# Converting weight pieces two at a time: 1024 columns per operation in place of 512

## The chip, the cores and the metric

The kernel runs on one core of a Trainium2 chip. A core has five instruction streams that run side by side and wait for each other on semaphores: TensorE (PE in the profile; PEld is its weight loading), VectorE (DVE), ScalarE (ACT), GpSimd (POOL) and SyncE (SP, which here issues the transfers). The metric is device time in microseconds, the median of several runs; lower is better. The inputs of the three runs before are the same.

## The reference

Two blocks run one after the other. An attention without softmax, with 8 batches, 8 heads, 576 positions and 64 features per head, each row divided by its root mean square:

```
kv  = einsum('bhsd,bhse->bhde', k, v)
out = einsum('bhsd,bhde->bhse', q, kv)
out = out / sqrt(mean(out*out, -1) + 1e-6) * g_norm
```

and a feed-forward block on its 4608 rows of 512 features, with 2048 hidden features:

```
x = out.transpose(0, 2, 1, 3).reshape(4608, 512)
y = maximum(x @ w_in, 0)**2 @ w_out
```

The two weight matrices arrive as 64-bit floats, and the kernel must make 32-bit floats of them on the chip: it takes the two 32-bit words of each number as integers and puts sign, exponent and fraction together with shifts and masks.

## The kernel before, in words

The rows are worked through in nine strips of 512. Strip 0 is multiplied plainly, strip 1 with seven products in place of eight (sums of blocks of operands are prepared for that), later strips with two such levels. Everything is emitted by one Python program; each engine then executes its own instructions strictly in the order in which they were emitted, and the semaphore waits between engines are put in by a framework that tracks which stretch of a tile each instruction reads and writes.

**The weights.** There are 32 pieces of 128 x 512 numbers: pieces 0 to 15 of `w_in`, in four groups g of four (kc = 0 to 3), pieces 16 to 31 of `w_out`. A piece takes two operations on ScalarE (the magnitude of the high word into `w_c`, line 254; the low word shifted, in place in `raw`, line 258) and four on VectorE (clip, line 266; shift and mask, 268; sign, 272; the final integer add, 275, a custom instruction that writes the result). Pieces 0 to 3 are converted one by one among the work on the first strip (`first_piece`). The other 28 are converted in pairs, numbered here 2 to 15, by `convert_pieces`: ScalarE is one pair ahead, and on VectorE the eight operations of the two pieces alternate, so that no operation directly follows the one whose result it needs. Pairs 2 to 7 belong to `w_in`, 8 to 11 to the first half of `w_out` (`pieces_out`), 12 to 15 to its second half (`sums_out`), and behind each of these last four come eight subtractions of 256 columns (`minus`, line 292) and four stores of the sums to device memory (line 325).

**The result tile.** `w_in` has the layout `[partition, kh, g, block, 256 columns]`, with kh = 0 or 1, g = 0 to 3 and seven blocks; blocks 0 to 3 hold the four quarters of the weight, and blocks 4 to 6 sums and pieces of `w_out`. Within a partition all of kh = 0 lies ahead of all of kh = 1. A pair of `w_in` is one block range of one group g at both kh.

**The readers.** The up projection of strip 0 has 16 steps, called slots here (`up_first`, four slots for each g, 2 halves fh by 2 column blocks i). A slot multiplies four chunks of 128 input features (kc 0 to 3, in this order; kc % 2 is kh) into one of four PSUM buffers (tags A, B, A, C) at line 900, and ScalarE squares the positive part of the sum (lines 905 and 907) before the buffer can be used again four slots on. Slots 0 to 2 are finished early (`first_up`). The conversion of a pair is emitted between slots: pairs 2, 3, 4 and 5 behind slots 0, 1, 2 and 3, pairs 6 to 11 ahead of slots 4 to 9, pair 12 behind slot 11 and pairs 13 to 15 behind slots 13 to 15. ScalarE's two operations for pair n + 1 are emitted at the place of pair n.

**Buffers and queues.** `raw` has 8 buffers of one piece each, which the last four pairs share for their sums (`wt`); `w_c` has 4. Every load of a piece and every store goes through SP's one queue in program order; a load waits until its buffer is free.

Behind the up projection come the down projection of strip 0 (line 859, from 83.76 us), the sums `g_s` for it, and the sums of the weights for later strips (`w_t`), all of which VectorE does right behind the last pair.

Of the kernel before, what the change touches and what calls it, by code (L numbers as in the profile page):

```python
# [10 lines left out]
FP32 = mybir.dt.float32  # L11
I32 = mybir.dt.int32
U32 = mybir.dt.uint32
I64 = mybir.dt.int64
AF = mybir.ActivationFunctionType
ALU = mybir.AluOpType
# [4 lines left out]
def kernel(  # L21
# [34 lines left out]
    nc = tc.nc  # L56
    P = 128
# [4 lines left out]
    NP = H // 2  # L62
# [27 lines left out]
    c_pool = ctx.enter_context(tc.tile_pool(name="c", bufs=6))  # L90
    conv = ExitStack()
    xt_pool = conv.enter_context(tc.tile_pool(name="xt", bufs=1))
    raw_pool = conv.enter_context(tc.tile_pool(name="raw", bufs=8))
    spare_pool = conv.enter_context(tc.tile_pool(name="spare", bufs=1))
    wtmp = conv.enter_context(tc.tile_pool(name="wtmp", bufs=4))
    psums = ExitStack()
    fpsum = psums.enter_context(tc.tile_pool(name="fpsum", bufs=4, space=bass.MemoryType.PSUM))
    opening = ExitStack()
# [110 lines left out]
    def drip_queries():  # L209
# [5 lines left out]
    KH, FH, DH = NP // 2, d_ff // 2, d_model // 2  # L215
    FQ = FC // 2
    WN = 512
    NG = FQ // 2

    w_in = wpool.tile([P, KH, NG, 7, WN // 2], FP32, name="w_in")  # L220

    w_out = dram.tile([7, P, 2, FQ, P], FP32, name="w_out")
# [5 lines left out]
    w_out_11, w_out_21, w_out_t1 = w_first = [  # L228
        w_in[:, :, :, b].rearrange("p k g e -> p (k g) e") for b in (4, 5, 6)
    ]  # L230
    w_in_v = moe_w_in.rearrange("(kc p) (b g f) -> kc g p b f", p=P, b=2, g=NG)
    w_out_v = moe_w_out.rearrange("(b j p) (eh e) -> eh j p b e", p=P, b=2, eh=2)
    sources = [w_in_v[kc, g] for g in range(NG) for kc in range(NP)]
    sources += [w_out_v[eh, j] for eh in range(2) for j in range(FQ)]
    raw = []

    def load_piece():
        if len(raw) < len(sources):
            t = raw_pool.tile([P, 2, WN // 2], I64, name="raw", tag="raw")
            nc.sync.dma_start(out=t, in_=sources[len(raw)])  # L240
            raw.append(t)


    LEAST, MOST = 2.0**-15, float.fromhex("0x1.DFFFFEp+16")

    words, acted = {}, [0]

    def convert_on_act(i, parts=(0, 1)):
        view = lambda dt: raw[i].bitcast(dt).rearrange("p b (n two) -> p b n two", two=2)
        low, high, high_f = view(U32)[:, :, :, 0], view(I32)[:, :, :, 1], view(FP32)[:, :, :, 1]  # L250
        r = view(I32)[:, :, :, 0]
        if 0 in parts:
            c = wtmp.tile([P, 2, WN // 2], FP32, name="w_c", tag="w_c")
            nc.scalar.activation(c, high_f, AF.Abs)  # L254
            words[i] = c, r, high

        if 1 in parts:
            nc.scalar.activation(r, low, AF.Copy, scale=2.0**-29)  # L258

    def conversion(i, dest, eng=nc.vector):  # L260

        c, r, high = words.pop(i)
        ci = c.bitcast(I32)


        yield eng.tensor_scalar(out=c, in0=c, scalar1=LEAST, scalar2=MOST, op0=ALU.max, op1=ALU.min)

        yield nc.vector.tensor_scalar(
            out=ci, in0=ci, scalar1=3, scalar2=0x3FFFFFFF, op0=ALU.logical_shift_left, op1=ALU.bitwise_and
        )  # L270

        yield nc.vector.scalar_tensor_tensor(
            out=ci, in0=high, scalar=-(2**30), in1=ci, op0=ALU.bitwise_and, op1=ALU.bitwise_or
        )
        yield nc.vector.tensor_tensor(out=dest.bitcast(I32), in0=ci, in1=r, op=ALU.add)

    def convert_pieces(ids, dests):

        for i in range(acted[0], min(ids[-1] + 3, len(sources))):
            convert_on_act(i)  # L280
            acted[0] = i + 1
        for _ in zip(*[conversion(i, dest) for i, dest in zip(ids, dests)]):
            pass
        load_more(ids[-1] + 1)

    def load_more(end):

        while len(raw) < min(end + 8, max(len(sources) - 4, end + 4), len(sources)):
            load_piece()

    def minus(eng, out, a, b):
        eng.tensor_tensor(out=out, in0=a, in1=b, op=ALU.subtract)  # L292

    def pieces_in(i):
        g, kc = divmod(i, NP)
        b = kc // KH * 2
        convert_pieces((i, i + 1), [w_in[:, kh, g, b : b + 2] for kh in range(KH)])

    def sums_in(g):

# [5 lines left out]
        minus(nc.vector, a21, a11, a21)  # L306

    def pieces_out(j):
        dest = lambda j: w_in[:, j // NG, j % NG, 4:6]
        convert_pieces((NG * NP + j, NG * NP + j + 1), [dest(j), dest(j + 1)])  # L310

    def sums_out(j):
        js = (j, j + 1)
        t = [raw_pool.tile([P, 4, DH], FP32, name="wt", tag="raw") for _ in js]
        convert_pieces([NG * NP + FQ + j for j in js], [x[:, 0:2, :] for x in t])
        for x, j in zip(t, js):
            minus(nc.vector, w_out_t1[:, j, :], x[:, 0], w_out_11[:, j, :])
        for x, j in zip(t, js):
            minus(nc.vector, x[:, 2], x[:, 1], w_out_t1[:, j, :])
        for x in t:  # L320
            minus(nc.vector, x[:, 0], x[:, 1], x[:, 0])
        for x, j in zip(t, js):
            minus(nc.vector, x[:, 3], w_out_21[:, j, :], x[:, 2])
            for e in range(2):
                nc.sync.dma_start(out=w_out[3:7, :, e, j].rearrange("b p e -> p b e"), in_=x[:, :, ts(e, P)])

    conversions = [(pieces_in, i) for i in range(0, NG * NP, 2)]
    conversions += [(pieces_out, j) for j in range(0, FQ, 2)] + [(sums_out, j) for j in range(0, FQ, 2)]
    converted = [NP // 2]

# [25 lines left out]
    for p in range(2, NP):  # L356
        load(0, p, nc.sync, "q")
        load_piece()
        load(0, p, nc.sync, "kv")
        next(to_load)  # L360
# [239 lines left out]
    def first_piece(i, n):  # L600

        if i not in first_steps:
            first_steps[i] = conversion(
                i, w_in[:, i % KH, 0, i // KH * 2 : i // KH * 2 + 2], nc.gpsimd if i else nc.vector
            )
        for _ in range(n):
            next(first_steps[i])
# [74 lines left out]
    def sums_x(s):  # L682
# [10 lines left out]

    act, T, K, Q, N, F, piece = (
        convert_on_act, transposed_query, key_value, first_queries, first_normalized, first_features, first_piece
    )
    U = first_up
    size, low = (lambda i: (act, (i, (0,)))), (lambda i: (act, (i, (1,))))
# [7 lines left out]
    def query_pairs(b):  # L706
        first_n = b // 2 * PAIR + (C if b % 2 else 0)
        ns = list(range(first_n, first_n + C + b % 2))
        return [ns[i : i + 2] for i in range(0, len(ns), 2)]
# [9 lines left out]
    T, K, last = transposed_query, key_value, query_pairs(1)[2]  # L719
# [624 lines left out]
    attend(ready[0])  # L1344
    opening.close()
    apsum = psums.enter_context(tc.tile_pool(name="apsum", bufs=2, space=bass.MemoryType.PSUM))
    for i in range(NP, NP + 2):
        convert_on_act(i)
    acted[0] = NP + 2
    for s in range(N_STRIP):  # L1350
        attend(ready[s])
        if s == DEEP_UP - 1:
# [23 lines left out]
        for i, (w, fn, a) in enumerate(steps):  # L1376
# [33 lines left out]
            if s:  # L1410
                clock[0] += 3.2 if i >= n_up else 2.2 if s == DEEP else 1.2
                soon = tiles_due and tiles_due[0][2][0] // NT == s + 1
                if i == n_up + 10:
                    while tiles_due and tiles_due[0][2][0] // NT == s + 1:
                        _, f, a = tiles_due.popleft()
# [38 lines left out]
            n = i + 1 - (n_up - 6)  # L1454
# [44 lines left out]
```

## Time and profile before

| what | us |
|---|---|
| three runs | 871.0, 872.37, 872.51 |
| median | 872.37 |
| span of the profiled execution, first to last instruction | 867.8 |
| TensorE busy in it | 858.3 (99%) |
| VectorE busy | 721.5 (83%) |
| ScalarE busy | 352.1 (41%) |
| strip 0's slots and the conversions, in the span | about 31 to 95 |

The page gives the span of the profiled execution and no separate whole time for it; the median of the timed runs is 4.6 us more than the span, which is what lies around the program. The timeline view lists the instructions of one engine in order of time: start in us, time in us, engine, line, operation, result <- operands, forms, number of instructions merged, and in square brackets the idle time ahead of it and what ended it. Instructions overlap in the pipeline: the distance from start to start is what counts, the time shown is longer. A matmul of 32-bit operands appears as two instructions.

### The profile page before, as it was taken

What the parts mean: (1) busy time and instruction counts of PE and PEld (TensorE: products, weight loads), DVE (VectorE), ACT (ScalarE), POOL (GpSimd) and SP (SyncE); (2) the same over time, 40 slices, a digit from 0 to 9 for tenths busy, and PEclk for the clock granted to TensorE, in tenths of its full rate; (3) what the DMA queues carried; (4) which work ended last, traced back from release to release, by engine and by line L of the source; (5) the groups of instructions that cost most, each with busy time, mean ns of one, the idle gap of its engine ahead of it and who ended that gap; (6) DMA issues with size and microseconds to landing.
All of it is one profiled execution on the core that took longest, in us unless ns stands there. A gap on an engine that the chain in (4) does not pass through costs nothing.

```text
span 867.8 us, 32590 instructions
## 1 busy us (share of the span) xinstructions
PE 858.3 (99%) x14176; PEld 803.7 (93%) x14176; DVE 721.5 (83%) x1236; ACT 352.1 (41%) x805; POOL 316.2 (36%) x321
## 2 busy tenths in 40 slices
PE   8999999999999999999999999999999999999998
PEld 7445888889999999999999999999999999999998
DVE  3999998879887996789689977897889777975887
ACT  5799251320048303750356034901491148102810
POOL 1100003630459223730574045704470447145700
PEclk9999999999999999999999999999999999999999
DMA  9998997999999997989788979997668856885583
GB/s 312 301 335 251 288 376 233 296 323 361 276 261 261 346 328 235 232 311 336 213 244 272 336 244 258 294 317 260 213 221 300 305 161 220 291 286 195 177 311 124
DMA packets 169470, 236.47 MB, mean 273 GB/s; under 512 B 78704, under 2 KB 133744, under 8 KB 161008
## 3 DMA queue, kind: packets, MB, share of 16 engines
q1 hardware_dynamic: 169024, 234.33, 83.6%
q8 instruction: 111, 1.82, 0.9%
q14 instruction: 31, 0.25, 0.1%
q10 hardware_dynamic: 304, 0.07, 0.0%
HBM read 197.66 MB, written 36.70 MB: 270 GB/s over the span
## 4 chain that ended last, share of the span: by engine, by line
PE 83%; DVE 7%; ACT 5%; DMA 4%; issue 1%; SPq 0%; DVEq 0%; ACTq 0%
PE ps_A L854 35%; PE ps_B L854 31%; PE ps_C L854 5%; PE ps_A L859 4%; PE kv_ps L437 2%; PE x_ps L473 2%; PE ps_B L859 2%; DVE w_t L292 1%; ACT raw L258 1%; ACT w_c L254 1%; DMA w_blk<-w_deep 1%; DMA w_deep<-w_t 1%; DVE wt L292 1%; DMA first_qkv<-in_v_dram 1%; DMA raw<-in_moe_w_out_dram 1%
## 5 line engine op out<-in xcount | busy, mean ns | idle before, releaser
L854 PE MATMUL ps_B<-w_blk,g_s 128*64 128x128 f32 x2016 | 122.0, 273 | 0.0
L854 PEld LDWEIGHTS ps_B<-w_blk,g_s 128*64 128x64 f32 x2016 | 112.6, 137 | 0.1
L854 PE MATMUL ps_A<-x_l,w_in 128*64 128x128 f32 x1568 | 102.4, 273 | 0.6 <-ACT snap L1317 0.6
L292 POOL TENSOR_TENSOR x_l<-xT 128x256 f32<-128x256 f32 x21 | 16.0, 764 | 230.9 <-PE ps_A L854 230.9
L854 PE MATMUL ps_B<-w_blk,gt 128*64 128x128 f32 x1504 | 94.1, 273 | 0.9 <-DMA w_blk<-w_deep 0.9
L854 PE MATMUL ps_A<-w_blk,g_s 128*64 128x128 f32 x1536 | 92.2, 273 | 0.0
L854 PEld LDWEIGHTS ps_A<-x_l,w_in 128*64 128x64 f32 x1568 | 88.9, 137 | 0.9 <-ACT snap L1317 0.8
L1312 POOL TENSOR_TENSOR snap<-snap,gt 128x512 f32<-128x512 f32 x35 | 46.3, 1322 | 112.3 <-ACT snap L1317 102.7
L854 PEld LDWEIGHTS ps_B<-w_blk,gt 128*64 128x64 f32 x1504 | 84.6, 137 | 1.4 <-PE ps_B L854 1.1
L854 PEld LDWEIGHTS ps_A<-w_blk,g_s 128*64 128x64 f32 x1536 | 85.7, 137 | 0.0
L1317 ACT COPY snap<-ps_A 128x512 f32<-128x512 f32 x63 | 36.9, 585 | 103.8 <-PE ps_A L854 96.6
L1252 ACT ACTIVATE gt<-gt 128x512 f32<-128x512 f32 x112 | 70.1, 626 | 9.5 <-DVE gt L1312 9.5
L1253 ACT ACTIVATE gt<-gt 128x512 f32<-128x512 f32 x112 | 70.7, 631 | 3.6
L854 PE MATMUL ps_A<-w_blk,gt 128*64 128x128 f32 x1152 | 71.2, 273 | 0.0
L1101 ACT COPY o_sb<-ps_A 128x128 f32<-128x128 f32 x24 | 6.4, 266 | 144.9 <-PE ps_A L854 115.5
L854 PEld LDWEIGHTS ps_A<-w_blk,gt 128*64 128x64 f32 x1152 | 64.7, 137 | 0.0
L1100 DVE TENSOR_TENSOR o_sb<-o_sb,ps_B 128x256 f32<-128x256 f32 (+1 forms) x123 | 47.4, 386 | 15.0 <-ACT o_sb L1101 9.8
L292 DVE TENSOR_TENSOR gt<-gt 128x2048 f32<-128x2048 f32 (+1 forms) x29 | 59.7, 2063 | 0.0
L1312 POOL TENSOR_TENSOR gt<-gt,snap 128x512 f32<-128x512 f32 x42 | 52.6, 1283 | 15.0 <-DVE snap L1312 15.0
L854 PE MATMUL ps_B<-x_l,w_blk 128*64 128x128 f32 x784 | 51.2, 273 | 0.0
L854 PE MATMUL ps_A<-x_l,w_blk 128*64 128x128 f32 x784 | 51.2, 273 | 0.0
L1101 ACT COPY o_sb<-ps_B 128x128 f32<-128x128 f32 x31 | 8.3, 266 | 96.5 <-PE ps_B L854 96.5
(196 smaller groups left out, 1836.5 us busy)
## 6 DMA issues: line engine op xcount, KB each, us to landing
w_blk<-w_deep SPq DMA_DIRECT2D x56, 1024.0 KB, 7.4
w_blk<-w_out SPq DMA_DIRECT2D x56, 768.0 KB, 6.6
w_blk<-w_in_deep SPq DMA_DIRECT2D x49, 768.0 KB, 5.9
raw<-in_moe_w_in_dram SPq DMA_DIRECT2D x16, 512.0 KB, 7.4
raw<-in_moe_w_out_dram SPq DMA_DIRECT2D x16, 512.0 KB, 4.9
k<-in_k_dram SPq DMA_DIRECT2D x29, 256.0 KB, 5.4
v<-in_v_dram SPq DMA_DIRECT2D x29, 256.0 KB, 6.0
x_d<-x_q SPq DMA_DIRECT2D x27, 256.0 KB, 5.2
```

The costliest lines, as they stand in the source:

```text
L254: nc.scalar.activation(c, high_f, AF.Abs)
L292: eng.tensor_tensor(out=out, in0=a, in1=b, op=ALU.subtract)
L437: nc.tensor.matmul(ps[ts(h, D), i], lhsT=a, rhs=w, start=i == 0 and c == 0, stop=c == C, skip_group_check=True)
L473: nc.tensor.matmul(ps[half, r, i, ts(p, D)], lhsT=q[row, half], rhs=kvd[b, p][row, row], start=True, stop=True)
L854: nc.tensor.matmul(ps[half], lhsT=lhsT[:, half], rhs=rhs, start=start, stop=stop, skip_group_check=True)
L859: nc.tensor.matmul(bank[BANK[p]][:, i, :], lhsT=lhsT(k), rhs=rhs(k), start=p in (1, 5, 2) and i == 0 and k == 0, stop=k == n - 1, skip_gro ...
L1100: add = lambda out, a, b: nc.vector.tensor_tensor(out=out, in0=a, in1=b, op=ALU.add)
L1101: yield nc.scalar.copy(q[:, 3:4], small(1))
L1252: nc.scalar.activation(o, o, AF.Relu)
L1253: nc.scalar.activation(o, o, AF.Square)
L1312: add = lambda eng, out, a, b: eng.tensor_tensor(out=out, in0=a, in1=b, op=ALU.add)
L1317: nc.scalar.copy(t, ps)
```

## The change

`raw` becomes 4 buffers of a pair each and `w_c` 2, the same bytes as before. Pieces 0 to 3 are converted as before. From piece 4 on a pair is one thing: two operations on ScalarE and four on VectorE, each over 1024 columns, on the engines where they were; the final add writes both halves of the pair with one instruction whose result is a strided view of `w_in` (`side`): for pieces of `w_in` both kh at one g, for pieces of `w_out` two neighbouring g at one kh. The sums of the last four pairs become four subtractions of 512 columns for a pair, and they are emitted one pair later, behind the conversion of the next pair (`left_out`). The order of everything else in the program stays.

```diff
-    raw_pool = conv.enter_context(tc.tile_pool(name="raw", bufs=8))
+    raw_pool = conv.enter_context(tc.tile_pool(name="raw", bufs=4))
-    wtmp = conv.enter_context(tc.tile_pool(name="wtmp", bufs=4))
+    wtmp = conv.enter_context(tc.tile_pool(name="wtmp", bufs=2))
...
+            if i % 2 == 0:
+                raw_pairs.append(raw_pool.tile([P, 2, 2, WN // 2], I64, name="raw", tag="raw"))
+            t = raw_pairs[i // 2][:, i % 2]
+            nc.sync.dma_start(out=t, in_=sources[i])
...
+    def convert_pair_on_act(n):
+        view = lambda dt: raw_pairs[n].bitcast(dt).rearrange("p a b (n two) -> p a (b n) two", two=2)
+        c = wtmp.tile([P, 2, WN], FP32, name="w_c", tag="w_c")
+        act_words(c, view)
+        pair_words[n] = c, view(I32)[..., 0], view(I32)[..., 1]
...
-        yield nc.vector.tensor_tensor(out=dest.bitcast(I32), in0=ci, in1=r, op=ALU.add)
-
-    def convert_pieces(ids, dests):
-
-        for i in range(acted[0], min(ids[-1] + 3, len(sources))):
-            convert_on_act(i)
+        yield add_eng.tensor_tensor(out=dest.bitcast(I32), in0=ci, in1=r, op=ALU.add)
+
+    def convert_pair(n, dest, add_eng=nc.vector):
+
+        for i in range(acted[0], min(n + 2, len(sources) // 2)):
+            convert_pair_on_act(i)
             acted[0] = i + 1
-        for _ in zip(*[conversion(i, dest) for i, dest in zip(ids, dests)]):
-            pass
-        load_more(ids[-1] + 1)
+        deque(conversion(pair_words.pop(n), dest, add_eng=add_eng), 0)
+        load_more(2 * n + 2)
...
+    side = lambda t: t.rearrange("p a b e -> p a (b e)")
...
-        convert_pieces((i, i + 1), [w_in[:, kh, g, b : b + 2] for kh in range(KH)])
+        convert_pair(i // 2, side(w_in[:, :, g, b : b + 2]))
...
-        dest = lambda j: w_in[:, j // NG, j % NG, 4:6]
-        convert_pieces((NG * NP + j, NG * NP + j + 1), [dest(j), dest(j + 1)])
+        k, g = divmod(j, NG)
+        convert_pair((NG * NP + j) // 2, side(w_in[:, k, g : g + 2, 4:6]))
...
+        x = raw_pool.tile([P, 2, 4, DH], FP32, name="wt", tag="raw")
+        last = j + 2 == FQ
+        convert_pair((NG * NP + FQ + j) // 2, side(x[:, :, 0:2, :]), nc.vector)
+        left_out.append((x, slice(j, j + 2)))
+        while len(left_out) > (0 if last else 1):
+            left_sums(*left_out.pop(0))
+
+    def left_sums(x, js):
+        minus(nc.vector, w_out_t1[:, js, :], x[:, :, 0], w_out_11[:, js, :])
+        minus(nc.vector, x[:, :, 2], x[:, :, 1], w_out_t1[:, js, :])
+        minus(nc.vector, x[:, :, 0], x[:, :, 1], x[:, :, 0])
+        minus(nc.vector, x[:, :, 3], w_out_21[:, js, :], x[:, :, 2])
+        for i in range(2):
             for e in range(2):
-                nc.sync.dma_start(out=w_out[3:7, :, e, j].rearrange("b p e -> p b e"), in_=x[:, :, ts(e, P)])
+                nc.sync.dma_start(out=w_out[3:7, :, e, js.start + i].rearrange("b p e -> p b e"), in_=x[:, i, :, ts(e, P)])
...
-    for i in range(NP, NP + 2):
-        convert_on_act(i)
-    acted[0] = NP + 2
+    convert_pair_on_act(NP // 2)
+    acted[0] = NP // 2 + 1
```

## The prediction, made before the changed kernel ran

> **What bounds the kernel now.** I read the busy totals and the chain of waits first, then the timeline of strip 0's up projection (31 to 95 us), where the whole change lies, and last the instruction list of the built changed kernel, which shows its waits but no times.
>
> ```profile
> span 867.8 us, 32590 instructions
> PE 858.3 (99%) x14176; PEld 803.7 (93%) x14176; DVE 721.5 (83%) x1236; ACT 352.1 (41%) x805; POOL 316.2 (36%) x321
> PE 83%; DVE 7%; ACT 5%; DMA 4%; issue 1%; SPq 0%; DVEq 0%; ACTq 0%
> ...
> 33.69 3.60 PE L900 MATMUL ps_C<-xT,w_in 128*128 128x512 f32 x8
> 37.12 1.88 PE L900 MATMUL ps_A<-xT,w_in 128*128 128x512 f32 x4
> 39.22 1.98 PE L900 MATMUL ps_A<-xT,w_in 128*128 128x512 f32 x4 [0.22 <-DVE w_in L275]
> 41.05 3.60 PE L900 MATMUL ps_B<-xT,w_in 128*128 128x512 f32 x8
> 55.23 3.70 PE L900 MATMUL ps_B<-xT,w_in 128*128 128x512 f32 x8 [0.29 <-ACT gt L907]
> 131.80 7.17 PE L859 MATMUL ps_A<-w_blk,gt 128*128 128x256 f32 x32 [0.26 <-DVE o_sb L1031]
> ```
>
> TensorE is busy 99% and carries the end. A slot takes 37.12 - 33.69 = 3.43 us, a chunk 0.857. From 31 to 132 us TensorE loses about 1.5 us to all waits: 0.22 at 39.22, 0.46 around 55.23, 0.11 at 58.77, 0.40 at 70.77, 0.36 around 131.80. No gain of this change can exceed that; a new wait of TensorE counts whole.
>
> **The change, part by part.**
>
> VectorE, four operations for eight:
>
> ```profile
> 25.52 0.42 DVE L268 TENSOR_SCALAR w_c<-w_c 128x512 int32<-128x512 int32 x1
> 25.97 0.69 DVE L272 SCALAR_TENSOR_TENSOR w_c<-raw,w_c 128x512 int32<-128x512 int32 x1
> 26.80 0.69 DVE L275 CUSTOM_DVE_ANT_0 w_in<-raw,w_c 128x1024 uint16<-128x1024 uint16 x1
> ...
> 35.94 0.76 DVE L266 TENSOR_SCALAR w_c<-w_c 128x512 f32<-128x512 f32 x2
> 36.61 0.76 DVE L268 TENSOR_SCALAR w_c<-w_c 128x512 int32<-128x512 int32 x2
> 37.28 1.29 DVE L272 SCALAR_TENSOR_TENSOR w_c<-raw,w_c 128x512 int32<-128x512 int32 x2
> 38.48 1.29 DVE L275 CUSTOM_DVE_ANT_0 w_in<-raw,w_c 128x1024 uint16<-128x1024 uint16 x2
> 39.69 0.42 DVE L266 TENSOR_SCALAR w_c<-w_c 128x512 f32<-128x512 f32 x1
> ```
>
> A pair takes 39.69 - 35.94 = 3.75 us: four starts 0.335 apart, four 0.60 apart. The lead-in of an operation is about 0.067, so 1024 columns cost 2 x 0.335 - 0.067 = 0.602 and 2 x 0.60 - 0.067 = 1.134. But each operation now directly follows the one whose result it needs. The first three lines of the fence, one piece alone, price that: shift to sign 25.97 - 25.52 = 0.45 (0.115 over 0.335), sign to final add 0.83 (0.23 over 0.60; 0.03 on another row, I take 0.19). A pair after: 2 x 0.602 + 2 x 1.134 + 2 x 0.115 + 0.19 = 3.89 us, with bounds 3.47 (dependence free) and 3.93. I take 3.89, as those rows are the same operations. A pair's sums: four subtractions, 4 x 0.602 + 0.115 = 2.53 for 8 x 0.335 = 2.68.
>
> [...]
>
> ScalarE: four operations 0.565 apart (34.07, 34.63) become two of 1.02 to 1.13; I take 1.03, the slope to a 2048-column row of 1.93. It saves 0.2 us per pair, but VectorE gets its first operand only when both pieces are done: pair 2's starts at 30.66 + 1.13 = 31.8. The relu and squares of a slot are 1.18 (36.32 to 37.52).
>
> The result view, which decides. A final add now writes both kh of one group with one instruction. Dependences go by the stretch between its first and last element, which in `[kh, g, block]` runs from (kh 0, g) to (kh 1, g) and covers other groups' chunks: kh 0 of later g, kh 1 of earlier g. The built program shows it, up projection of slots 3 to 6:
>
> ```
> L918 Matmult ps_C<-xT,w_in 128x512 [waits PE_49]
> L918 Matmult ps_C<-xT,w_in 128x512 [waits DVE_49]
> L918 Matmult ps_C<-xT,w_in 128x512 x2
> L918 Matmult ps_A<-xT,w_in 128x512 [waits Activation_49]
> L918 Matmult ps_A<-xT,w_in 128x512 [waits DVE_49]
> L918 Matmult ps_A<-xT,w_in 128x512 x2
> L918 Matmult ps_B<-xT,w_in 128x512 [waits Activation_49]
> L918 Matmult ps_B<-xT,w_in 128x512 [waits DVE_49]
> L918 Matmult ps_B<-xT,w_in 128x512 x2
> L918 Matmult ps_A<-xT,w_in 128x512 [waits DVE_49]
> ```
>
> Followed to the counts they ask for: slot 3's second chunk waits for the final add of pair 4 (before: no VectorE wait in slot 3), slot 4's second chunk for pair 6, slot 5's for pair 7, slot 6's first for pair 8, slot 12 for pairs 9 and 11. None of these numbers is read there. Before, slot 4 waited for pairs 2 and 3, slot 8 for 4 and 5, slot 12 for 6 and 7. TensorE is in order, so everything behind the second chunk of slot 3 stops. In return the final adds of pairs 5, 7, 8 and 10 wait for chunks of slots 3, 4, 5 and 7.
>
> The chain, with pairs of 3.89:
> - pairs 2, 3, 4 end at 35.7, 39.6, 43.5. Slot 3 runs its first chunk 33.69 to 34.55, then stands until 43.6: idle 9.1.
> - After such a stop the clock is unknown. The only cold start in the trace is the program's:
>
> ```profile
> 1.35 3.25 PE L381 MATMUL t_ps<-ident 128*128 128x128 f32 x14 [1.35 <-POOL ident masks.py:199]
> 6.99 0.71 PE L381 MATMUL x_ps<-ident 128*128 128x128 f32 x4
> ```
>
> There the same instructions stood 0.22 us apart first and 0.11 later, for about 3.3 us. I take that restart here: three chunks end at 47.9 (at full speed 46.2).
> - ScalarE's operations for pair 6 stand behind the relu of slot 3 (to 49.2), so pair 6 starts at 50.35 and ends at 54.2; slot 4's second chunk starts at 54.4: idle 5.7. Again 3.3 us at half speed: slot 4 ends at 58.6.
> - pair 7's add waits for slot 4's third chunk and ends at 59.0: some 0.5 of wait in slot 5, which ends at 62.1.
> - pair 8 starts behind slot 4's relu, at 61.1, and ends at 65.0: slot 6 starts at 65.1, idle 3.1, restart at full speed taken. Slots 6 and 7 end at 68.6 and 72.0.
> - Before, slot 7 ended at 51.34: +20.7. The waits at 55.23, 58.77, 70.77 and 131.80 are covered then: -1.3. **Sum +19.4 us.**
>
> Without the clock term slot 7 ends at 68.8: gaps 9.1, 5.7, 0.5 and 2.6, +16.1. With 5 us of half speed, or also behind the third gap, it comes to +21 to +23.5. These are the ends of the range.
>
> [...] No run here yet shows a mid-program stop.
>
> What else moves, at nothing because of TensorE's new delay:
> - VectorE ends its conversions at about 113.6 for 95.4, +18.2. What follows has the old slack and 1.2 more: `g_s` ready at 116.1 where TensorE needs it at 119.8; o_sb (131.06) at 149.3 for 151.2. Without that cover a microsecond at most.
> - Pairs' stores: the `wt` buffer of pair 14 is that of pair 12, whose four stores now issue a pair later, some 2.5 us ahead of the reuse (before about 9). They land 5.4 to 5.7 us after issue (75.9 to 81.3 before): pair 14's add stalls VectorE 1.2 us inside the cover, 3 without. The pairs' sums behind it wait.
> - SP: the loads of pieces 30 and 31 go ahead of pair 12's stores, and twelve stores, for eight, stand at the end; the `w_blk` loads that need them follow 2.2 to 4.4 us after, where TensorE has its 19 us. Raw loads wait for a whole pair's buffer and ScalarE for both its pieces; the last, 14 and 15, landed at 46.8 and 48.75 before, when ScalarE waited 0.57 for them, and are needed about 15 us later now. The loads of later strips' k, v and q in the same queue stand behind TensorE too, and hold back only loads with that slack.
> - `w_c`, two pairs: ScalarE is one pair ahead, as before.
>
> The profiled span is 867.8 and the median 872.37 (4.6 more, outside the program); the delta is worked out in the span, and I add it to the median: 872.37 + 19.4 = **891.8 us**. A measurement of this kernel can tell about 0.2% (1.7 us) from no change.
>
> **The rivals.**
> 1. The stops restart at full speed: +16.1, 888.5 us. For it: granted clock 9 in every slice of the page, and nothing in the trace that stops TensorE after its start. Against: the cold start at 1.35.
> 2. Half speed lasts longer or comes at the third gap too: 893.4 to 895.9.
> 3. Dependence on VectorE is free: pairs of 3.47 end earlier by 0.42 each, 1.3 at slot 3 and 0.4 at each later gap, of which some 2.1 reach the end: 889.7. Against: 0.45 against 0.335.
> 4. Not slower: the waits are already met when the matmuls arrive, and VectorE's lead-ins saved free TensorE's 1.5: 870.9. It decides if pair 4 is done by 34.8, so that slot 3's second chunk starts with less than 0.3 idle. Against: pair 4's last add could not end before 42.2 even at 3.47 a pair.
> 5. Conversions slow down but the waits count for little (readers late anyway): the dependence alone, 28 x 0.14 / 2 = 2 us, and the stores 3 uncovered: 874 to 878.
>
> **How the numbers follow.** Main chain 0.55, rival 1 0.2, rival 2 0.12, rival 3 0.05, rival 4 0.04, rival 5 0.04. The forecast is the main chain. The range holds main, 1, 2 and 3: 0.92 before the spread of the bases, so 887 to 896. Not slower comes from rival 4 and the low end of 5 alone: slower 0.95, same 0.03, faster 0.02.
>
> **What would show it.** Right: slot 3's second chunk at line 918 idle about 9 us, ended by VectorE `w_in`; slot 4's 5.7; ahead of slot 6 about 3; chunk spacing 1.7 for 0.857 behind the first two; a pair 3.9 apart on VectorE; VectorE idle some 3 us for ScalarE ahead of pair 6; pair 14's add ended by a store of `wt`; the wait at 131.80 gone. Wrong: TensorE running through slot 3 at 34.55, pairs nearer 3.5, clock unchanged behind a gap, or a loss behind 95 us: then the covers above failed.

## The result, and the profile after

The changed kernel takes 893.27 us (median of four runs, 892.13 to 900.21) where the kernel before takes 871.68 in the same comparison: slower by a factor of 1.0273, 95% interval 1.0235 to 1.0312. The forecast was 891.8, with a range of 887 to 896.

The profiled execution is the slowest of the four, 900.21 us. Some 6.5 us of it are three stalls of TensorE between 273 and 290 us (0.79, 0.95 and 3.03 us) that the profile puts down to nothing ("issue"), and a half clock behind them (290.7 to 294.1 us at a granted 0.50, which costs 1.7). Without them it would be near the other three. The losses read below lie ahead of that. The busy totals of the changed kernel's page:

```profile
span 898.1 us, 32446 instructions
PE 866.8 (97%) x14176; PEld 808.3 (90%) x14176; DVE 721.9 (80%) x1164; ACT 349.2 (39%) x777; POOL 314.5 (35%) x321
```

VectorE has 72 instructions fewer and as much busy time; TensorE's share falls from 99% to 97%. Where, the timeline of TensorE in the changed kernel tells (start, time, line, operation; in brackets the idle time ahead and what ended it):

```profile
33.26 1.02 PE L918 MATMUL ps_C<-xT,w_in 128*128 128x512 f32 x2
43.41 5.26 PE L918 MATMUL ps_C<-xT,w_in 128*128 128x512 f32 x6 [9.14 <-DVE w_in L288]
48.51 1.02 PE L918 MATMUL ps_A<-xT,w_in 128*128 128x512 f32 x2
55.12 4.53 PE L918 MATMUL ps_A<-xT,w_in 128*128 128x512 f32 x6 [5.59 <-DVE w_in L288]
...
61.05 2.84 PE L918 MATMUL ps_B<-xT,w_in 128*128 128x512 f32 x6 [0.55 <-DVE w_in L288]
66.13 3.70 PE L918 MATMUL ps_A<-xT,w_in 128*128 128x512 f32 x8 [2.23 <-DVE w_in L288]
...
125.37 1.32 PE L661 MATMUL xt_ps<-ident,x_n 128*128 128x128 f32 x8 [0.37 <-DVE x_n L586]
132.83 7.17 PE L877 MATMUL ps_A<-w_blk,gt 128*128 128x256 f32 x32 [1.60 <-DVE gt L304]
```

Slot 3 does one chunk and stands 9.14 us until the final add of pair 4 is done (it starts on VectorE at 42.13); slots 4, 5 and 6 follow with 5.59, 0.55 and 2.23. The forecast had 9.1, 5.7, 0.5 and 3.1. The last two lines are new: in this execution TensorE waits for VectorE behind the first down projection too, 2 us in all, which the forecast had not.

The three chunks behind the first two stops take 5.1 and 4.4 us, where three chunks take 2.6 at other places. The view by stretches shows why (stretch in us, its length, busy time and instructions of PE, PEld, DVE, ACT and POOL, the granted clock, DMA share, GB/s):

```profile
38.07:43.41 5.34, 0.00 (x0) 0.00 (x0) 5.02 (x6) 4.08 (x6) 0.00 (x0) 0.50 0.97 304
43.41:48.31 4.90, 4.89 (x6) 2.19 (x7) 2.47 (x3) 0.00 (x0) 0.00 (x0) 0.50 1.14 308
48.31:51.72 3.41, 1.22 (x3) 0.19 (x1) 1.92 (x2) 2.98 (x5) 0.00 (x0) 1.00 1.03 276
51.72:55.12 3.40, 0.00 (x0) 0.00 (x1) 3.20 (x4) 2.37 (x3) 0.00 (x0) 0.50 0.83 305
55.12:58.55 3.43, 3.43 (x4) 1.50 (x5) 2.47 (x3) 0.00 (x0) 0.00 (x0) 0.50 0.72 226
```

The clock is halved from 38.07 to 48.31 us and from 51.72 to 58.55, so for 4.90 and 3.43 us in which TensorE works.

VectorE's pairs, and the wait that leads to the two late losses (timeline of VectorE in the changed kernel, pair 4 and then the end of pair 14):

```profile
39.33 0.68 DVE L279 TENSOR_SCALAR w_c<-w_c 128x1024 f32<-128x1024 f32 x1
40.05 0.69 DVE L281 TENSOR_SCALAR w_c<-w_c 128x1024 int32<-128x1024 int32 x1
40.77 1.23 DVE L285 SCALAR_TENSOR_TENSOR w_c<-raw,w_c 128x1024 int32<-128x1024 int32 x1
42.13 1.23 DVE L288 CUSTOM_DVE_ANT_0 w_in<-raw,w_c 128x2048 uint16<-128x2048 uint16 x1
43.28 0.69 DVE L279 TENSOR_SCALAR w_c<-w_c 128x1024 f32<-128x1024 f32 x1
...
105.94 1.23 DVE L288 CUSTOM_DVE_ANT_0 wt<-raw,w_c 128x2048 uint16<-128x2048 uint16 x1 [3.73 <-DMA w_out<-wt]
```

A pair takes 43.28 - 39.33 = 3.95 us (3.75 before, 3.89 forecast): start to start 0.72, 0.72, 1.36 and 1.15. For the stretch behind the down projection, these are the lines of the kernel before, of the run with the sums at once and of the run with two stops filled (both below):

```profile
109.61 7.17 PE L859 MATMUL ps_A<-w_blk,gt 128*128 128x256 f32 x32
129.71 7.17 PE L877 MATMUL ps_A<-w_blk,gt 128*128 128x256 f32 x32
128.57 7.17 PE L877 MATMUL ps_A<-w_blk,gt 128*128 128x256 f32 x32 [0.26 <-DVE gt L304]
```

The opening of the program differs by itself from one execution to the next: slot 3 starts anywhere from 32.2 to 35.6 us in the profiles below, and the whole time differs with it. So this table gives each profile's distance from its own start of slot 3, as the difference to the kernel before (where the four distances are 17.65, 50.07, 75.92 and 98.11 us). Each row's distances come from one execution; "fourth" is the fourth `w_blk` product:

| kernel | slot 8 | down projection | first `w_blk` product | fourth | median us (before beside it) | ratio, 95% |
|---|---|---|---|---|---|---|
| changed | +22.2 | +21.2 | +23.7 | +23.5 | 893.27 (871.68) | 1.0235 to 1.0312 |
| split adds | +2.7 | +2.5 | +5.8 | +5.6 | 875.45 (870.69) | 1.0040 to 1.0089 |
| merged add alone | +22.4 | +21.4 | +21.7 | +21.6 | 891.85 (870.69) | 1.0229 to 1.0263 |
| split adds, `w_in` alone | +18.6 | +17.7 | +18.0 | +17.9 | 890.00 (869.29) | 1.0206 to 1.0261 |
| busy in two stops | +19.8 | +18.9 | +19.1 | +19.0 | 888.67 (870.69) | 1.0194 to 1.0230 |
| busy in three stops | +18.1 | +17.2 | +17.1 | +17.1 | 889.01 (870.71) | 1.0174 to 1.0230 |
| sums at once | +21.8 | +20.9 | +20.8 | +20.4 | 890.11 (870.69) | 1.0208 to 1.0245 |
| split adds, sums at once | +1.1 | +2.5 | +3.3 | +3.7 | 874.11 (869.29) | 1.0029 to 1.0067 |
| the same, ScalarE by pieces | +1.7 | +2.4 | +2.5 | +3.2 | 873.27 (869.29) | 1.0030 to 1.0058 |
| halves, ScalarE by pieces, sums at once | +1.3 | +1.4 | +1.3 | +0.9 | 870.89 (869.29) | 1.0008 to 1.0036 |
| `raw` in pairs alone | +0.5 | +0.7 | +0.7 | +0.8 | 870.45 (870.71) | 0.9984 to 1.0019 |

### The profile page after: what moved, and what is told of

Its sections match the earlier page's. It is cut to its first block, busy times and chain, and to the rows that moved or that the text cites. A ratio compares the mean times of both kernels' runs of the same rounds, so it can differ in the third digit from the quotient of the medians.

```text
span 898.1 us, 32446 instructions
## 1 busy us (share of the span) xinstructions
PE 866.8 (97%) x14176; PEld 808.3 (90%) x14176; DVE 721.9 (80%) x1164; ACT 349.2 (39%) x777; POOL 314.5 (35%) x321
## 4 chain that ended last, share of the span: by engine, by line
PE 83%; DVE 9%; DMA 3%; ACT 2%; issue 1%; SPq 1%; DVEq 0%
PE ps_A L872 34%; PE ps_B L872 30%; PE ps_C L872 4%; PE ps_A L877 4%; PE kv_ps L455 2%; PE x_ps L491 2%; PE ps_A L918 2%; PE ps_B L877 2%; PE ps_C L918 1%; DVE w_t L304 1%; DMA v<-in_v_dram 1%; DVE w_c L285 1%; DVE wt L304 1%; DMA first_qkv<-in_v_dram 1%; DVE gt L304 1%
## 5 line engine op out<-in xcount | busy, mean ns | idle before, releaser
L1330 POOL TENSOR_TENSOR gt<-gt,snap 128x512 f32<-128x512 f32 x42 | 52.5, 1280 | 21.8 <-DVE snap L1330 21.8
L1076 DVE TENSOR_TENSOR g_s<-gt 128x512 f32<-128x512 f32 x56 | 46.4, 829 | 0.0
```

The lines of the kernel that those rows point to most:

```text
L1076: nc.vector.tensor_tensor(out=t, in0=a21, in1=a22, op=ALU.add)
L1330: add = lambda eng, out, a, b: eng.tensor_tensor(out=out, in0=a, in1=b, op=ALU.add)
```

## The experiments

### The strided result, taken away

```diff
-        yield add_eng.tensor_tensor(out=dest.bitcast(I32), in0=ci, in1=r, op=ALU.add)
+        for a in parts:    # the two halves of a pair
+            yield add_eng.tensor_tensor(out=dest[:, a].bitcast(I32), in0=ci[:, a], in1=r[:, a], op=ALU.add)
```

> The changed kernel with the last operation of a pair cut in two adds of 512 columns, each with a result that lies in one piece; everything else stays 1024 wide. Theory A (TensorE's new waits on the strided result cost nearly all of the 21.6 us): no stop in slot 3, slots 3 to 7 run as before with some 0.3 us of wait in slot 4. What stays is VectorE: a pair 0.725 + 0.725 + 1.365 + 2 x 0.60 = 4.02 us for 3.75, 14 pairs are 3.8 us, and pair 14's wait for stores 2 to 4 us more; that reaches TensorE behind the first down projection, where the changed kernel lost 2 us to VectorE: 877 to 880 us. Theory B (the wide operations themselves cost it, by their chain of dependent results): stays at 892 to 894.

875.45 us, below the 877 to 880 of theory A: of the 21.6 us against the kernel before, 4.8 are left, though clip, shift and sign are still 1024 wide. TensorE in slots 3, 4 and 8 of this kernel:

```profile
33.02 3.60 PE L919 MATMUL ps_C<-xT,w_in 128*128 128x512 f32 x8
38.72 1.98 PE L919 MATMUL ps_A<-xT,w_in 128*128 128x512 f32 x4 [0.39 <-DVE w_in L289]
53.38 3.70 PE L919 MATMUL ps_A<-xT,w_in 128*128 128x512 f32 x8 [2.38 <-ACT gt L926]
```

Slot 3 runs through and slot 4 waits 0.39 us for pair 3. What is left of the loss, 4.8 us, is in places that the stops of the changed kernel had covered. One was not expected: 2.38 us ahead of slot 8. Its buffer is freed by ScalarE's relu of slot 4, which stands behind pair 7's wide operation, started at 49.98 us; before, the first piece of that pair was taken at 46.92 and the second at 48.75. This wait is not the same in every execution (see the run with split adds and the sums at once). Theory B (the wide operations cost it) would have left the time at 892 to 894, and is out.

### The strided result alone

```diff
+        ops = [conversion([t[:, a] for t in of], dest[:, a]) for a in range(2)]
+        for _ in range(3):          # clip, shift, sign: 512 columns, the halves alternating
+            for op in ops:
+                next(op)
+        add_eng.tensor_tensor(out=dest.bitcast(I32), in0=of[0].bitcast(I32), in1=of[1], op=ALU.add)
```

> The opposite part alone: on VectorE clip, shift and sign of a pair are again six operations of 512 columns that alternate between its halves, and only the final add is one of 1024 columns with the strided result. Theory A: the stops are all there (slot 3 about 8.5 us idle, slot 4 about 5.5, slot 6 about 2.5), since a pair ends only 0.15 to 0.2 us sooner: 891 to 893 us. Theory B: back near the kernel before, 872 to 876.

891.85 us, all four stops are there (two of them shown), and 22.4 us are lost by slot 8:

```profile
42.60 5.49 PE L923 MATMUL ps_C<-xT,w_in 128*128 128x512 f32 x6 [8.99 <-DVE w_in L300]
54.49 4.72 PE L923 MATMUL ps_A<-xT,w_in 128*128 128x512 f32 x6 [5.49 <-DVE w_in L300]
```

The two runs are each other's complement: one instruction's result view makes the stops, and the width of the other three makes almost none of them.

### Half of the false waits

The adds are split for pairs 2 to 7 only:

```diff
-        deque(conversion(pair_words.pop(n), dest, add_eng=add_eng), 0)
+        deque(conversion(pair_words.pop(n), dest, add_eng=add_eng, parts=(0, 1) if n < 8 else (slice(None),)), 0)
```

> The changed kernel with the two contiguous adds for pairs 2 to 7 only; pairs 8 to 11 (pieces of w_out) keep the strided add. Theory A: slots 3, 4 and 5 run through, but slot 6's first chunk still asks for pair 8, which ends at about 59.2 us by the run with all adds split, so slot 6 stands from 44.0 to 59.3 in place of three shorter stops, restarts at half clock (about 2.5 us), and covers the later waits again: 886 to 890 us. If the false waits cost by their number or only those of w_in matter: 877 to 880.

890.00 us, at the upper end of what theory A gave. Slots 3 to 5 run through but for 0.39 us in slot 4, then slot 6 stands from 43.4 us until pair 8 is done:

```profile
58.61 6.61 PE L919 MATMUL ps_A<-xT,w_in 128*128 128x512 f32 x8 [15.25 <-DVE w_in L289]
```

With fewer false waits the loss by slot 8 is 18.6 us for 22.2. False waits on a pipeline of pairs aren't additive: what counts is the latest pair that the earliest reader asks for. Mending half of them would have looked like a failed idea.

### The clock in the stops

Matmuls of the identity, which nobody reads, are put into the stops: 40 in slot 3 and 24 in slot 4, behind their first chunk.

```diff
+                if kc == 0 and slot in (3, 4):
+                    warm = apsum.tile([P, NP, P], FP32, name="warm", tag="at")
+                    keep_busy(warm[:, 0], 40 if slot == 3 else 24)
```

> The changed kernel with matmuls of the identity that nobody reads in the two long stops: 40 in slot 3, 24 in slot 4, behind the chunk ahead of the stop (8.8 and 5.3 us at the 0.22 us that such a matmul takes at full clock), so that TensorE is not idle there. If the granted clock of one half (38.1 to 48.3 and 51.7 to 58.6 us in the changed kernel) comes from the idle time, it stays at 1.0, the three chunks behind each stop take 2.6 us for 5.1 and 4.4, and all behind comes about 4.3 us sooner: 889 us (888 to 890). If the chunks are slow for another reason: no gain, 893 or more.

888.67 us. The chunks behind both stops run at full speed again (2.68 and 2.67 us start to start for 5.10 and 4.36), but slot 6 does not. TensorE's timeline, then its stretches (length, busy, granted clock, DMA share, GB/s), of this kernel:

```profile
43.68 2.84 PE L918 MATMUL ps_C<-xT,w_in 128*128 128x512 f32 x6 [0.20 <-DVE w_in L288]
...
62.32 5.40 PE L918 MATMUL ps_A<-xT,w_in 128*128 128x512 f32 x8 [2.24 <-DVE w_in L288]
67.56 3.60 PE L918 MATMUL ps_C<-xT,w_in 128*128 128x512 f32 x8
```

```profile
59.77:63.18 3.41, 1.17 (x3) 1.00 0.49 185
63.18:66.59 3.41, 3.41 (x5) 0.50 0.84 305
```

Slot 6 takes 5.24 us for 3.43: the stop is as long as the one that cost nothing more in the changed kernel (2.24 us for 2.23), and here the granted clock is 0.50 from 63.18 to 66.59 us. A half clock is not in every execution of this kernel: by estimate one half-clock stretch of 3.41 us takes 0.002 off the granted clock of the whole span (0.5 x 3.41 of 889.0), which is 0.998 in two of the four timed executions, this one among them, and 1.0 in the other two. The third stop was filled as well, with nine more ahead of slot 6:

```diff
+            if 4 * g + 2 * fh + i == 6:
+                warm = apsum.tile([P, NP, P], FP32, name="warm", tag="at")
+                keep_busy(warm[:, 0], 9)
             for kc in range(NP):
```

> As the run with matmuls of the identity in the two long stops, and nine more (2.0 us) ahead of slot 6, where that run fell to half clock from 63.2 to 66.6 us behind an idle time of only 2.24 us, so that slot 6 took 5.24 us for 3.43. If the idle time is the cause, the clock stays whole through all the slots, slot 6 takes 3.43 us, and the whole 1.8 us less: 886 to 887.5 us. If slot 6 was slow for another reason, it stays at 888.7. What is left to the kernel before is then the waits themselves, some 17 us.

In the profile it is as expected: slot 6 takes 3.54 us and slots 7 and 8 3.44 and 3.43, the full speed, and slot 8 comes 1.7 us sooner than with two stops filled (+18.1 for +19.8). The time doesn't show it: 889.01 us, 885.01 to 889.77, above the 886 to 887.5 expected. In the profiled execution the opening was 2 us later (slot 3 at 35.55 us for 33.52), and its granted clock is 0.998 over the whole span. With two stops filled the granted clock says that only two of the four executions had a half-clock stretch at all, so the other two had no 1.8 us to save. What the profiles of the two runs do give is the split of the loss at slot 8: 22.2 us are 18.1 of waits and 4.1 of half clock.

### The sums at once

```diff
-        while len(left_out) > (0 if last else 1):
+        while left_out:
```

> The changed kernel with each pair's sums and stores right behind its own conversion, not a pair later. If the 2 us that TensorE loses behind the first down projection (0.4 ahead of the x_n transposes, 1.6 for gt) come from pair 14's add waiting 3.7 us for the stores of pair 12, those stores now issue some 9 us sooner, the wait goes, VectorE is 4 to 6 us earlier there and 1.9 to 2.3 us come back: 890.5 to 891.5 us. If they come from elsewhere (the wide subtractions, late loads), it stays within 0.5 us of the changed kernel.

890.11 us, somewhat below the 890.5 to 891.5 expected, and both late waits are gone. From the down projection to the first `w_blk` product the changed kernel takes 28.3 us; here it is 25.8 (129.71 - 103.93), as before (25.9). Pair 14's add follows its sign operation without a wait (99.67 to 101.02 us, 100.99 to 105.94 in the changed kernel). In that execution the 2.4 us come by way of the wait of pair 14's add for stores that issue a pair later.

But later sums need not cost this. The strided add alone, half of the false waits and the two runs with filled stops have them too, and take 26.2, 26.2, 26.1 and 25.8 us for the same stretch (128.57 - 102.46 = 26.1 with two stops filled). There pair 14's add waits 1.38 to 2.72 us, in two of them for a store and in two for ScalarE, and starts 0.65 to 2.02 us ahead of the down projection; in the changed kernel it starts 1.37 us behind it (105.94 against 104.57), and with split adds, where the stretch takes 29.1 us, 2.09 behind. So the loss goes by how late that add comes to TensorE, up to about 0.3 us where it is early and 2.4 to 3.2 where it is late, and the profiles show one execution of each kernel. The timed runs don't decide it: 1.0208 to 1.0245 here against 1.0235 to 1.0312.

### Toward the kernel before, part by part

Split adds and the sums at once (the diffs of these two runs together):

> The changed kernel with the two contiguous adds and also with each pair's sums and stores right behind its own conversion. With the two adds alone TensorE still lost 2.4 us ahead of slot 8 (a buffer that ScalarE frees late), 1.2 ahead of the x_n transposes and 1.6 for gt, 4.8 us against the kernel before. If the last two come from pair 14's add, which waited 3.1 us for stores, they go nearly whole and the 2.4 stays: 872.5 to 873.5 us. If they come from VectorE's longer pairs (14 x 0.27 = 3.8 us) and not from the stores, little changes: 875.

874.11 us, above the 872.5 to 873.5 expected. In the profile 2.4 us go behind the down projection, as with the strided adds (+3.3 for +5.8 at the first `w_blk` product); the rest lies in smaller waits for VectorE and ScalarE up to there. The 2.38 us ahead of slot 8 are 0.75 here, though the two kernels do the same up to that place. ScalarE's operation for pair 7 starts 15.3 us behind slot 3 (48.04, after 2.77 us of waiting for a load of `raw`), where it was 17.0 with split adds alone. So the wait ahead of slot 8 differs by 1.6 us between two executions of the same work. By the down projection both are +2.5. The whole time moved by less than the intervals can tell (1.0029 to 1.0067 against 1.0040 to 1.0089), so the gain is seen in the stages of the profile and not in the timed runs.

ScalarE by pieces too:

```diff
-        act_words(c, view)
+        for a in range(2):
+            act_words(c[:, a], lambda dt: view(dt)[:, a])
```

> As the last, and ScalarE's two operations of a pair are again four of 512 columns, piece by piece, with VectorE still 1024 wide. If the 2.4 us ahead of slot 8 come from ScalarE waiting for both pieces of pair 7 (its first operation started at 49.98 for 46.92 and 48.75, and the relu that frees the buffer stands behind it), they fall back to the 0.3 to 0.5 of the kernel before: 870.5 to 871.8 us, 2 us below the last. If ScalarE was late for want of a w_c buffer, the wait stays and so does the time of the last.

873.27 us, above what was expected. The wait ahead of slot 8 is 0.96 us, between the 0.75 and 2.38 of the two profiles with the wide operation, so what ScalarE's width does to it can't be told. (The 0.3 to 0.5 of the kernel before is ahead of slot 9; ahead of slot 8 it has no wait.)

Then VectorE's halves as well, so that only the buffers of a pair and the wide sums remain:

```diff
-        deque(conversion(pair_words.pop(n), dest, add_eng=add_eng), 0)
+        of = pair_words.pop(n)
+        ops = [conversion([t[:, a] for t in of], dest[:, a], add_eng=add_eng) for a in range(2)]
+        for _ in range(4):
+            for op in ops:
+                next(op)
```

> What is left of the change without its three costs: VectorE's four operations of a pair in halves that alternate, ScalarE by pieces, sums and stores at once. It keeps the buffers of a pair and the sums in four subtractions of 512 columns, 0.15 us less VectorE time per pair at the end of the conversions. TensorE had lost 0.36 us there to VectorE in the kernel before (at 131.80), so the gain is at most that: 870.2 to 871.2, no difference that can be told. If pair buffers or the wide sums cost something of their own: 872 or more.

870.89 us, inside the 870.2 to 871.2 expected, though slower than the kernel before by 0.08 to 0.36%; 1.18 us are lost ahead of slot 8. ScalarE in this kernel, with the idle time ahead of pieces 14 and 15:

```profile
47.52 0.68 ACT L255 ACTIVATE w_c<-raw 128x512 f32<-128x512 f32 x1 [1.71 <-DMA raw<-in_moe_w_in_dram]
49.20 0.68 ACT L255 ACTIVATE w_c<-raw 128x512 f32<-128x512 f32 x1 [0.43 <-DMA raw<-in_moe_w_in_dram]
50.35 0.59 ACT L928 ACTIVATE ps_A<-ps_A 128x512 f32<-128x512 f32 x1
```

ScalarE waits for the loads of pieces 14 and 15. By the program the first load into a pair's buffer now waits for the final add of both pieces that held it, not of one. Last, that alone in the kernel before, all operations as they were:

```diff
-    raw_pool = conv.enter_context(tc.tile_pool(name="raw", bufs=8))
+    raw_pool = conv.enter_context(tc.tile_pool(name="raw", bufs=4))
...
-            t = raw_pool.tile([P, 2, WN // 2], I64, name="raw", tag="raw")
+            if len(raw) % 2 == 0:
+                raw_pairs.append(raw_pool.tile([P, 2, 2, WN // 2], I64, name="raw", tag="raw"))
+            t = raw_pairs[-1][:, len(raw) % 2]
...
-        t = [raw_pool.tile([P, 4, DH], FP32, name="wt", tag="raw") for _ in js]
+        pair = raw_pool.tile([P, 2, 4, DH], FP32, name="wt", tag="raw")
+        t = [pair[:, 0], pair[:, 1]]
```

> The kernel before with one thing of the change: raw in four buffers of a pair in place of eight of a piece, so that a pair's first load waits for the last add of the pair that held the buffer. All operations are those of the kernel before. If the wait ahead of slot 8 in the run with halves (1.2 us, ScalarE waiting 1.7 and 0.4 us for the loads of pieces 14 and 15) comes from that, it is here too: 0.8 to 1.4 us ahead of slot 8, 870 to 871 us where the kernel before has 869.3. If it comes from the w_c buffers or the sums: no difference.

870.45 us, 0.9984 to 1.0019: no difference that can be told. In the profile there is 0.38 us ahead of slot 8, less than the 0.8 to 1.4 expected, and 0.47 ahead of slot 9; against the kernel before it is 0.5 to 0.8 us in all. That is less than the 1.6 us by which the wait ahead of slot 8 differs between two executions of the same work, so whether the buffers of a pair cost anything is not shown, and what makes the 1.3 us of the run above is open.

No version here is faster than the kernel before. Its own waits between 31 and 132 us are 1.5 us, and no part of the change reaches them.

## Why the prediction was right, point by point

- **The strided result decides.** Right, and shown by the two complementary runs. It could be read before any run from the built program's waits and the counts they ask for; the profile of before had nothing of it.
- **The stops.** 9.1, 5.7, 0.5, 3.1 us forecast, 9.14, 5.59, 0.55, 2.23 measured. The last, ahead of slot 6, is shorter than forecast. Slot 4 ended 0.9 us later than assumed, mostly by the clock in slot 3, and that moved pair 8 as well (it starts at 62.00 for 61.1). What shortens the stop is pair 7's add: the prediction had it wait for slot 4's third chunk, but it starts at 59.77, behind the last (59.65), so slot 5 ends 1.8 us later and pair 8 only 1.1. In the same way pair 5's add stands 2.85 us until slot 3 ends, so VectorE's wait for ScalarE ahead of pair 6 is 1.00 us and not the 3 of the forecast.
- **The pair.** 3.89 forecast, 3.95 measured. The sum's terms hold: 0.72 for clip and for shift (0.602 + 0.115), 1.15 for the add. The lead-in of 0.067 in them is an estimate from such rows: a subtraction of 256 columns takes 0.335 before (start to start, 86.31 to 86.98 us for two), one of 512 columns 0.61 here, and 2 x 0.335 - 0.61 is 0.06. The under-sized one is sign to add, 1.36: I took 0.19 for the dependence, and it is the 0.23 of the upper row. The rival in which a dependence costs nothing falls: an operation that needs the result just ahead of it starts 0.72 us after it, and one that doesn't 0.61 (the subtractions of the sums, 512 columns: 107.08, 107.80, 108.41). Four operations take 3.95 us here where eight took 3.75.
- **The half clock.** That TensorE goes on at half speed behind the two long stops is right (granted clock 0.50), its term was mis-sized: twice 3.3 us of half speed, a loss of 3.3 us; measured 4.90 and 3.43 us, 4.3 us by the slots' lengths and 4.1 by the runs with filled stops. The restart is not a fixed time (last section). That slot 6 restarts at full speed behind 3.1 us is a term that no run shows: the stop was 2.23 us, and slot 6 took 3.54 us behind it at a granted clock of 1.00, but 5.24 us behind 2.24 us with two stops filled.
- **Slot 7's end**, +20.7 us forecast, is +22.2 from slot 3's start: 1.0 of the difference is the clock; the rest, 0.5, is of the size of the longer pairs (0.06 each, seven of them ahead of slot 6) and was not taken apart.
- **"What follows has the old slack and 1.2 more" is a step that failed, in the profiled execution.** I checked the cover of `g_s` and of o_sb, and not of what VectorE does between them. x_n and gt (0.37 and 1.60 us of wait) had next to none: in the changed kernel VectorE ends its conversions 118.63 - 95.42 = 23.2 us later, and TensorE is 23.2 us later at the first `w_blk` product (132.83 - 109.61). The conversions' end came 5 us later than my 113.6. Half of that is pair 14's store wait, 3.73 us and not 1.2; some 1.5 are the later slots. The four stores issue behind four raw loads (91.44 to 95.20 us) and land some 9 us after the first, not 5.4 to 5.7. And those loads came late, for they stand on SP behind a k load that waited 16.9 us for TensorE. That is the step on "loads with that slack": the loads' slack was there for TensorE, not for ScalarE, which waited 1.08 us for one of them.
- **The terms put at nothing under TensorE's delay** are real where that cover is gone: 4.8 us in the run with split adds, of which the profiles give the stores some 2.4. The rival for the dependences and stores alone, 874 to 878, holds that run's 875.45, but partly by luck: 2.7 us of its profile lie ahead of slot 8, where ScalarE waits, and that rival has no such term.
- **The base.** "4.6 us outside the program" was wrong: 900.21 - 898.1 = 2.1 lie around the span, and the rest is spread between executions. As a difference was added to a median, it cost nothing: 21.6 us measured between the medians, 19.4 forecast. In the profile the terms add up to 20.7 + 1.5 (clock and pairs) - 1.0 (waits of before that are covered) + 2.4 (stores) = 23.6 for 23.5 at the fourth `w_blk` product; a wait of 0.9 us for w_blk later on in the kernel before is then covered too, and the rest of the difference to 21.6 is within what the openings differ by. The sum holds for this execution: four other kernels with late sums don't show the 2.4. Against the forecast of 19.4 all its errors point one way (1.5, 2.4, and 0.3 less covered than assumed), so the forecast did not come near by errors that cancel.

## What to carry to other kernels

When two writes are merged into one strided write, ask what the dependence tracker takes it to cover: here it is the stretch from first to last element, and readers of everything in between wait for it. Follow each new wait in the built program to the instruction that it asks for, and the stop can be worked out before anything runs: three of the four here came out within 0.11 us, and the last was off by 0.9, mostly for one wait read a chunk too early. A cover has to be checked for every consumer on the late engine, above all for the ones behind the first, and a mend has to be whole: half of the false waits still cost 18 of 22 us.

## What was not expected of the hardware

- **The half clock lasted whole multiples of 3.41 us, and the length of a stop alone did not set it.** The half-clock times behind stops are 10.24 us (38.07 to 48.31), 6.83 (51.72 to 58.55), 3.41 (63.18 to 66.59 with two stops filled) and 17.06 (47.43 to 64.49 with half of the false waits): 3, 2, 1 and 5 times 3.41. Slot 4's stop is 5.59 us long in the changed kernel and in the kernel with the sums at once; in the first the clock is halved for 6.83 us and in the second for 3.42 (last row below).
- **The 3.41 us ahead of a halving were not always idle.** The clock was halved behind stretches in which TensorE was busy 1.22 us of 3.41 (changed kernel, row from 48.31) and 1.17 (two stops filled, row from 59.77), and not behind ones with 1.46 and 1.94. Whether busy time draws the line, and where between these it would lie, is not shown. Three stretches in a row of the kernel with the sums at once:

```profile
47.55:50.96 3.41, 1.46 (x4) 0.38 (x2) 1.69 (x2) 2.74 (x5) 0.00 (x0) 1.00 0.91 273
50.96:54.37 3.41, 0.00 (x0) 0.00 (x0) 3.21 (x4) 2.61 (x3) 0.00 (x0) 1.00 0.83 296
54.37:57.79 3.42, 3.20 (x4) 1.51 (x5) 2.69 (x4) 0.00 (x0) 0.00 (x0) 0.50 0.63 208
```

The clock is still whole in the second, behind 1.46 us of work, and halved in the third, behind none. The two stops ahead of slot 6 differ in the same way: the one of 2.24 us with two stops filled cost 1.8 us more and began in the stretch with 1.17 us of work, the one of 2.23 us in the changed kernel cost nothing more and began in that with 1.94 (61.96 to 65.38). That it goes by how a stop falls into such stretches is my reading of these few.
- **Where the full clock came back, the 3.41 us before had been full of work, or nearly.** In the changed kernel work starts at 43.41, the clock is still halved behind the stretch from 41.48 to 44.90, in which TensorE is busy 1.49 us, and whole behind the next, which is all busy, to 48.31. In the last row above 3.20 us of work were enough; 2.47 were not, in the kernel with half of the false waits (57.66 to 61.08, work from 58.61). The work done at half speed behind a stop therefore differs: 3.20 us in the kernel with the sums at once, 3.43 and 4.90 in the changed kernel, 5.88 in the kernel with half of the false waits (58.61 to 64.49).
